# One table of issue orders for five engines: attention and two dense layers fused on one core

## The chip, the core and the metric

The kernel runs on one core of a Trainium2 chip. The core has five engines with a queue of instructions each: TensorE (PE in the profile), VectorE (DVE), ScalarE (ACT), GpSimd (POOL) and SyncE (SP), which issues every DMA of this kernel. An engine takes its instructions in the order in which they stand in its queue, and each of them waits on semaphores for what it reads and for the buffer it overwrites. The metric is the device time of one execution in microseconds (us); lower is better.

## The reference

```python
k_p = k.reshape(B, H, Sp, 8, D).mean(axis=3)          # B, H, S, D = 8, 8, 576, 64
v_p = v.reshape(B, H, Sp, 8, D).mean(axis=3)          # Sp = 72
scores = scale * np.matmul(q, k_p.transpose(0, 1, 3, 2))
attn = softmax(scores)
x = np.matmul(attn, v_p) -> reshaped to (4608, 512)   # one row for each token

h = x @ w_in                                          # 512 x 1024
solu = h * softmax(h)
ln = (solu - mean) / sqrt(var + 1e-06) * g_ln
x = ln @ w_out                                        # 1024 x 512

a, b = x @ w1, x @ w2                                 # 512 x 1024 each
out = (a * b) @ w3 @ w_out2                           # 1024 x 1024, 1024 x 512
```

## The kernel before

The program has two parts. The first holds the attention, the layer with `w_in` and `w_out`, and the conversion of `w1` and `w2`. It is cut into 18 units of 256 tokens, and each unit into 16 slots of PE work (`HEAVY = "hhhhxxxxHHHHyyyy"`: h chunks are products with `w_in`, L718; x chunks are products with `w_out`, L812 to L814). The attention of later tokens lies between them: scores `sc` (L582), maxima (L600), exponentials (L603), the division (`pr`, L623 and L630), transposes `pt` and `px` (L648, L651), and the product with the values, `av` (L687). Matrix products are made of a high and a low half of each operand (`xh` and `xl`, `gwh` and `gwl`, `pth` and `ptl`), so that each product is three matmuls.

q blocks come in 16 DMAs for each group of tokens (`qb`, L554), keys and values in `kv` tiles (L406, their remainder L414). The weights come as 64-bit words and are rounded to 32 bits by integer operations. A piece of 128 x 512 words is loaded into one of two buffers `f64` (`w_out` at L325, `w1` and `w2` at L247, "Kept" pieces; `w_in`, at the start, has six). POOL takes its low words (`cvm`, L258), ACT its magnitude (`cvb`, L260), DVE puts the bits together in three instructions (L263, L264, L267), and POOL adds the two (L273). A load into `f64` waits for L267 of the piece two before it. The 16 Kept pieces of `w1` and `w2` are then written back to DRAM (L359). `w_out` is centred over its rows: of each half of its columns four pieces are summed over the rows on PE (`nm`, L349), and L337 subtracts from it before it is split in `gwh` and `gwl`. The rows `h` go through `e` (L727, L733), are turned by PE (`lt`, L798) or through DRAM (`turn`, `ed`, `back`; L742, L749, L756), and each result `xo` is stored to `x2d` (L825).

The second part reads `x2d` back and forms `a` and `b` with seven products per block in place of eight (`p`, L1118 to L1120; their partial sums go to DRAM as `pd`, L1111), multiplies `w3` by `w_out2` (`ow`, L1277 to L1279), and ends in the last products (`o`, L1356 to L1358). `split` at L185 and L186 makes the high and the low half of an operand.

What sets the order: in the first part PE and SP issue in the order of the code (`manual_schedule` over the two), and DVE, ACT and POOL by the table `ISSUE_ORDER`, a list of offsets. In the second part all five engines issue in the order of the code. Nothing else is free: the tiles, the buffers and the operations are written out. Each DMA of SP also waits for the one that stands eight places before it in SP's queue, since eight semaphores take turns.

Of the kernel before, what the change touches and what calls it, by code (L numbers as in the profile page):

```python
# [1513 lines left out]
```

## Time and profile before

| | |
|---|---|
| three runs | 1217.00, 1218.17 and 1221.26 us, median 1218.17 us |
| profiled execution | 1221.05 us, its trace spans 1219.2 us |
| PE busy | 1163.4 us, 95% of the span |
| DVE, ACT, POOL busy | 895.7, 537.4, 522.5 us (73%, 44%, 43%) |
| DMA | 178.56 MB, mean 146 GB/s |
| granted clock of PE | 0.989 of full speed in the mean |

The span goes from the first to the last instruction. PE's 5% of idle time and its granted clock are where a change of order can act: the work itself stays. "SPq" in a view is SP's queue of DMAs. The clock of a stretch is the mean of two levels, full speed (2.4 GHz) and half of it.

### The profile page before, as it was taken

How to read it: one execution, taken by the hardware profiler on the slowest of the kernel's cores; microseconds unless marked ns; L12 is line 12 of the kernel's file. 1: busy time of each engine (PE TensorE's matmuls, PEld its weight loads, DVE VectorE, ACT ScalarE, POOL GpSimd, SP SyncE). 2: the span in 40 equal slices, each digit the busy share in tenths (PEclk: the TensorE clock that was granted, in tenths of full speed). 3: DMA queues.
4: the chain of work that ended last, by engine and by line, in shares of the span. 5: the costliest groups of instructions: out<-in, count | busy, mean ns of one | idle time of the engine just before them, and what ended most of it. 6: DMA issues, size and time to landing. Idle time of an engine off the chain costs nothing. (4 is left out here: it accounts for less than half of the span.)

```text
span 1219.2 us, 20186 instructions
## 1 busy us (share of the span) xinstructions
PE 1163.4 (95%) x7218; PEld 1037.5 (85%) x7218; DVE 895.7 (73%) x1376; ACT 537.4 (44%) x1399; POOL 522.5 (43%) x482
## 2 busy tenths in 40 slices
PE   7767999899999989999999999999999999999998
PEld 5656988788999989999999888888878887999997
DVE  6748777877887768658758977978784647877776
ACT  5544655565656566645533113131120224454534
POOL 3424333443344334200028657767672214645451
PEclk9989999999999999999999999999999999999999
DMA  9544255667677666435531642635612362153532
GB/s 234 116 113 96 70 126 139 187 163 192 168 193 204 173 146 197 127 133 184 176 126 61 220 164 98 205 130 180 201 61 86 121 216 86 49 195 122 181 131 87
DMA packets 167205, 178.56 MB, mean 146 GB/s; under 512 B 82624, under 2 KB 107200, under 8 KB 167104
## 3 DMA queue, kind: packets, MB, share of 16 engines
q1 hardware_dynamic: 167104, 177.26, 49.3%
q8 instruction: 57, 0.93, 0.3%
q14 instruction: 44, 0.36, 0.1%
HBM read 114.30 MB, written 62.91 MB: 145 GB/s over the span
## 5 line engine op out<-in xcount | busy, mean ns | idle before, releaser
L812 PE MATMUL x<-lnh,gwh 128*128 128x256 f32 x576 | 167.0, 290 | 0.0
L814 PE MATMUL x<-lnh,gwl 128*128 128x256 f32 x576 | 164.1, 285 | 0.0
L813 PE MATMUL x<-lnl,gwh 128*128 128x256 f32 x576 | 164.0, 285 | 0.0
L812 PEld LDWEIGHTS x<-lnh,gwh 128*128 128x128 f32 x576 | 111.1, 193 | 1.0 <-DVE lnl L802 0.2
L813 PEld LDWEIGHTS x<-lnl,gwh 128*128 128x128 f32 x576 | 111.2, 193 | 0.9
L603 ACT ACTIVATE ea<-sc,mx 128x72 f32<-128x72 f32 x320 | 98.0, 325 | 30.8 <-DVE mx L600 28.4
L814 PEld LDWEIGHTS x<-lnh,gwl 128*128 128x128 f32 x576 | 111.1, 193 | 0.0
L1122 ACT ACTIVATE p<-p 128x512 f32<-128x512 f32 (+1 forms) x40 | 22.2, 554 | 171.7 <-PE p L1120 165.1
L718 PE MATMUL h<-winh,xh 128*128 128x512 f32 x288 | 94.6, 410 | 1.8 <-DVE e L733 1.8
L1134 POOL TENSOR_TENSOR a<-a,b 128x512 f32<-128x512 f32 (+1 forms) x40 | 54.6, 1366 | 83.4 <-issue 57.3
L718 PE MATMUL h<-winl,xh 128*128 128x512 f32 x288 | 89.9, 393 | 0.0
L718 PE MATMUL h<-winh,xl 128*128 128x512 f32 x288 | 89.4, 392 | 0.0
L623 POOL TENSOR_TENSOR pr<-ea,sm 128x512 f32<-128x512 f32 x40 | 44.1, 1103 | 97.9 <-DVE sm L619 72.0
L727 ACT ACTIVATE e<-h,ST 128x1024 f32<-128x1024 f32 x36 | 40.2, 1116 | 64.8 <-DVE ST L726 64.5
L603 ACT ACTIVATION_READ_ACCUMULATOR ea<-sc,mx 128x1 f32 x320 | 67.8, 212 | 0.0
L718 PEld LDWEIGHTS h<-winh,xl 128*128 128x128 f32 x288 | 54.4, 189 | 12.1
L718 PEld LDWEIGHTS h<-winl,xh 128*128 128x128 f32 x288 | 54.4, 189 | 12.1
L1364 ACT ACTIVATE rows<-rows,kap 128x512 f32<-128x512 f32 x36 | 24.1, 716 | 90.3 <-DVE rows L1403 86.5
L1120 PE MATMUL p<-th,w1l 128*128 128x512 f32 (+1 forms) x160 | 59.4, 371 | 0.0
L1119 PE MATMUL p<-th,w1h 128*128 128x512 f32 (+1 forms) x160 | 59.1, 369 | 0.3 <-POOL th L1064 0.3
L1118 PE MATMUL p<-th,w1h 128*128 128x512 f32 (+1 forms) x160 | 59.3, 371 | 0.0
L1157 ACT ACTIVATE xq<-xq 128x512 f32<-128x512 f32 x24 | 16.2, 673 | 94.3 <-DMA xq<-in_moe_w_dram 65.8
(281 smaller groups left out, 3843.5 us busy)
## 6 DMA issues: line engine op xcount, KB each, us to landing
raw<-pd SPq DMA_DIRECT2D x18, 1024.0 KB
pd<-a SPq DMA_DIRECT2D x64, 256.0 KB
ed<-turn SPq DMA_DIRECT2D x28, 512.0 KB
back<-ed SPq DMA_DIRECT2D x112, 128.0 KB
x2d<-xo SPq DMA_DIRECT2D x35, 256.0 KB
kv<-in_k_dram SPq DMA_DIRECT2D x32, 256.0 KB
kv<-in_v_dram SPq DMA_DIRECT2D x32, 256.0 KB
f<-in_moe_w_dram SPq DMA_DIRECT2D x16, 512.0 KB
```

What stands on the lines that cost most here:

```text
L603: nc.scalar.activation(e[0:n, x], half[a][:, h], AF.Exp, bias=mx[0:n, x : x + 1], scale=1.0, accum_out=sm[0:n, x : x + 1],)
L623: nc.gpsimd.tensor_tensor(pr[0:n, 0 : H * KM].rearrange("p (h k) -> p h k", h=H), e[0:n, :, 0:KM], s8.to_broadcast([n, H, KM]), ALU.mult,)
L718: nc.tensor.matmul(self.ph[:, a], s_[:, c], w_[:, c, a * 512 : a * 512 + 512], start=first, stop=last)
L727: nc.scalar.activation(self.e, self.hv, AF.Exp, bias=st[:, 0:1], scale=1.0, accum_out=st[:, 1:2])
L812: nc.tensor.matmul(o, gw[0][:, f, ws], self.th[:, f], start=(f == 0), stop=False)
L813: nc.tensor.matmul(o, gw[0][:, f, ws], self.tl[:, f], start=False, stop=False)
L814: nc.tensor.matmul(o, gw[1][:, f, ws], self.th[:, f], start=False, stop=(f == FC - 1))
L1118: nc.tensor.matmul(o, wh[:, c, fsl], th[:, c], start=c == 0, stop=False)
L1119: nc.tensor.matmul(o, wh[:, c, fsl], tl[:, c], start=False, stop=False)
L1120: nc.tensor.matmul(o, wl[:, c, fsl], th[:, c], start=False, stop=c == 1)
L1134: nc.gpsimd.tensor_tensor(a[:, 0], a[:, 0], b[:, 0], ALU.mult)
L1364: nc.scalar.activation(dst, src, AF.Copy, scale=kap[:, n : n + 1])
```

## The change

The table now holds all five engines and the whole program, and the two `manual_schedule` blocks are gone. Its form is new too: runs of consecutive instructions (skip so many, take so many) in place of offsets. `issue_order` is called once, at the end, and chains the instructions of each engine in the table's order.

```diff
 def issue_order(tc, first):
     ins = list(tc.nc.cur_bb.bb.instructions)[first:]
     info = mybir.DependencyInfo(mybir.DependencyClass.NoSync, mybir.DependencyReason.DATA)
-    for engine, moves in ISSUE_ORDER.items():
-        traced = [i for i in ins if i.engine == getattr(mybir.EngineType, engine)]
-        order = [traced[k + m] for k, m in enumerate(moves)]
+    for engine, runs in ISSUE_ORDER.items():
+        traced = [i for i in ins if i.engine == getattr(mybir.EngineType, engine) and "Tile" not in type(i).__name__]
+        order, at = [], 0
+        for run in runs.split():
+            skip, _, count = run.partition(":")
+            at += int(skip)
+            order += traced[at : at + int(count or 1)]
+            at += int(count or 1)
+        assert len(order) == len(traced)
         for earlier, later in zip(order, order[1:]):
             tc.add_manual_dep(later, earlier.name, info, reason="issue order")
...
+    "SP": (
+        "0:2 2:2 -3 -2 3:3 1 -2 1 2 -3:2 5:2 -4:2 -4:2 4:6 2:2 -4:2 7:4 -9 8:8 4 -5:4 -20:4 17:2 3 -4 3:4 "
...
-    with tc.manual_schedule(engines={mybir.EngineType.PE, mybir.EngineType.SP}):
-        for s_ in range(min(events), SLOTS * (NU + 1) + 10):
+    for s_ in range(min(events), SLOTS * (NU + 1) + 10):
...
-    issue_order(tc, first_ins)
...
-    with tc.manual_schedule(engines={E.PE, E.SP, E.Activation, E.DVE, E.Pool}):
-        ON_POOL = (1, 3, 5)
+    ON_POOL = (1, 3, 5)
...
+    issue_order(tc, first_ins)
```

The instructions are the same ones on each engine: 6946 on PE, 1340 on DVE, 1007 on ACT, 485 on POOL and 792 on SP. On PE 344 of them stand in another place, nearly all in the first 245 us; on DVE 1196, on ACT 843, on POOL 359 and on SP 732. The new file is 25 to 28 lines longer, so L325 reads L352 there, L349 L376, L554 L581 and so on.

Three places, each of before and then of the change. The first is SP's queue at some 46 to 80 us, around the q blocks of the third group (`qb2`), the values of the second batch (`kv1_0`, `kv1_1`, `vl1`) and the pieces of `w_out` (`f64`). Before:

```order
26 L406 DMA kv1_0_635<-in_v_dram 64x2x512 x2
27 L414 DMA vl1_638<-in_v_dram 64x1x512 x2
28 L554 DMA qb2_641<-in_q_dram 32x8x32 x16
29 L325 DMA f64_683<-in_moe_w_out_dram 128x2x512
30 L406 DMA kv1_1_707<-in_v_dram 64x2x512 x2
31 L325 DMA f64_742<-in_moe_w_out_dram 128x2x512
32 L325 DMA f64_792<-in_moe_w_out_dram 128x2x512
33 L325 DMA f64_898<-in_moe_w_out_dram 128x2x512
34 L554 DMA qb3_928<-in_q_dram 32x10x32 x16
35 L325 DMA f64_989<-in_moe_w_out_dram 128x2x512
```

And now (`f64_681` is the piece that was `f64_683`; `f64_896` and `f64_987` were 898 and 989):

```order
27 L581 DMA qb2_639<-in_q_dram 32x8x32 x8
28 L352 DMA f64_681<-in_moe_w_out_dram 128x2x512
29 L581 DMA qb2_639<-in_q_dram 32x8x32 x4
30 L433 DMA kv1_0_633<-in_v_dram 64x2x512 x2
31 L441 DMA vl1_636<-in_v_dram 64x1x512 x2
32 L433 DMA kv1_1_705<-in_v_dram 64x2x512 x2
...
39 L581 DMA qb4_1294<-in_q_dram 32x8x32 x14
40 L433 DMA kv2_0_1141<-in_k_dram 64x2x512 x2
...
44 L441 DMA vl2_1291<-in_v_dram 64x1x512 x2
45 L352 DMA f64_896<-in_moe_w_out_dram 128x2x512
46 L352 DMA f64_987<-in_moe_w_out_dram 128x2x512
```

The q blocks and the fourth piece of `w_out` went ahead of the values of the second batch, and the last two pieces of `w_out` went behind the next group's q blocks and the third batch's keys.

The second place is PE's queue at some 112 to 130 us, at the row sums `nm` of the second half of `w_out`. Before:

```order
200 L349 MATMUL nm_1147<-cvb_820,gT_79 128x256 x2
201 L349 MATMUL nm_1147<-cvb_911,gT_79 128x256 x2
202 L349 MATMUL nm_1147<-cvb_1005,gT_79 128x256 x2
203 L349 MATMUL nm_1147<-cvb_1075,gT_79 128x256 x2
204 L812 MATMUL x2_0_0_1080<-lnh0_803,gwh_108 128x256
...
216 L687 MATMUL av2_2_1169<-pth2_953,VBDh_112 128x256
...
228 L718 MATMUL h1_1_1201<-winh_106,xh1_836 128x512 x2
```

And now, with the same names two or so lower:

```order
222 L376 MATMUL nm_1145<-cvb_818,gT_79 128x256 x2
223 L376 MATMUL nm_1145<-cvb_909,gT_79 128x256 x2
224 L714 MATMUL av2_2_1167<-pth2_951,VBDl_113 128x256
...
237 L745 MATMUL h1_1_1199<-winh_106,xh1_834 128x512 x2
238 L609 MATMUL sc3_0_1_1186<-bdt1_111,qT3_0_1070 128x144 x2
239 L376 MATMUL nm_1145<-cvb_1003,gT_79 128x256 x2
240 L745 MATMUL h1_1_1199<-winl_107,xh1_834 128x512 x2
...
245 L376 MATMUL nm_1145<-cvb_1073,gT_79 128x256 x2
246 L745 MATMUL h1_1_1199<-winh_106,xl1_835 128x512
```

The four pairs of sums stood in one row ahead of the x and h products; now the x products, `av2` and part of `h1_1` stand ahead of the third and the fourth pair.

The third place is DVE's queue at some 195 to 205 us of before, where the attention of the sixth group (`mx5`, `sm5`, `ptl5`) runs. Before, with one piece's conversion (`cvb_2127`) in it:

```order
259 L726 TENSOR_REDUCE ST_77<-h3_1_1982 128x1
260 L600 TENSOR_REDUCE mx5_1_2088<-sc5_1_0_2040 128x4
261 L438 TENSOR_REDUCE kp3_1_2147<-kv3_1_1979 128x128
262 L733 SCALAR_TENSOR_TENSOR e3_1_2031,ST_77<-h3_1_1982,e3_1_2031 128x1024
263 L600 TENSOR_REDUCE mx5_1_2088<-sc5_1_1_2043 128x4
264 L659 TENSOR_TENSOR ptl5_2115<-pt5_0_2117,pth5_2114 128x4x128
265 L660 TENSOR_TENSOR ptx5_2116<-px5_0_2122,ptx5_2116 64x128
266 L263 TENSOR_SCALAR cvb_2127<-cvb_2127 128x512
267 L742 STREAM_TRANSPOSE turn3_1_2063<-e3_1_2031 128x8x4x32
```

And now, from the same reduction of `h3_1` on:

```order
275 L753 TENSOR_REDUCE ST_77<-h3_1_1980 128x1
276 L627 TENSOR_REDUCE mx5_1_2086<-sc5_1_0_2038 128x4
277 L590 STREAM_TRANSPOSE qT6_1_2290<-qb6_2069 128x512
278 L290 TENSOR_SCALAR cvb_3304<-cvb_3304 128x512
279 L627 TENSOR_REDUCE mx5_1_2086<-sc5_1_1_2041 128x4
280 L291 TENSOR_SCALAR cvb_3304<-cvb_3304 128x512
281 L760 SCALAR_TENSOR_TENSOR e3_1_2029,ST_77<-h3_1_1980,e3_1_2029 128x1024
282 L686 TENSOR_TENSOR ptl5_2113<-pt5_0_2115,pth5_2112 128x4x128
283 L645 TENSOR_SCALAR sm5_1_2087<-sm5_1_2087 128x8
284 L646 RECIPROCAL sm5_1_2087<-sm5_1_2087 128x8
285 L294 SCALAR_TENSOR_TENSOR cvb_3304<-f64_3204,cvb_3304 128x512
```

The piece in this place is now a later one (3304; it was 3306, and DVE took it up at 304.7 us in before's trace, four pieces after 2127), and `qT6_1` came ahead by some rows. All 16 Kept pieces are taken up earlier in this way, at places that DVE reached by 275 us in before's trace, where the last of them was taken up at 502 us.

## Rows read from the trace of the kernel before

**Rows 1.** The page: PE's busy time, and DVE in 40 equal slices of the span.

```profile
PE 1163.4 (95%) x7218; PEld 1037.5 (85%) x7218; DVE 895.7 (73%) x1376; ACT 537.4 (44%) x1399; POOL 522.5 (43%) x482
...
DVE  6748777877887768658758977978784647877776
```

**Rows 2.** What PE waited for: total us, times, longest us.

```profile
PE nm L349 <- POOL cvb L273: 12.2, 2, 6.6
PE pkm L453 <- DMA kv<-in_k_dram: 7.3, 2, 6.4
...
PE sc L582 <- DVE xl L186: 3.2, 1, 3.2
PE w L313 <- DVE VBDl L186: 2.9, 1, 2.9
PE vs L444 <- DMA kv<-in_v_dram: 2.7, 1, 2.7
```

**Rows 3.** Stretches: length, busy us of each engine, PE's clock, DMA share, GB/s.

```profile
0.00:60.00 60.00, 46.36 (x248) 35.33 (x249) 41.49 (x83) 30.48 (x99) 23.57 (x42) 0.97 0.77 178
60.00:75.00 15.00, 12.85 (x83) 10.89 (x81) 6.86 (x20) 9.42 (x40) 5.02 (x10) 1.00 0.47 87
75.00:150.00 75.00, 60.63 (x366) 54.61 (x364) 56.75 (x112) 38.30 (x133) 26.55 (x34) 0.91 0.37 93
150.00:242.00 92.00, 85.43 (x564) 77.47 (x563) 68.67 (x128) 53.49 (x189) 38.74 (x55) 1.00 0.59 149
242.00:320.00 78.00, 74.64 (x496) 68.89 (x496) 56.82 (x95) 46.33 (x155) 26.02 (x37) 0.98 0.67 177
320.00:600.00 280.00, 276.55 (x1844) 255.53 (x1843) 206.26 (x346) 166.12 (x502) 83.03 (x117) 0.99 0.60 169
600.00:1000.00 400.00, 396.57 (x1980) 331.57 (x1979) 296.83 (x434) 93.51 (x147) 219.18 (x152) 1.00 0.43 144
1000.00:1050.00 50.00, 46.84 (x270) 40.06 (x269) 35.94 (x46) 24.12 (x43) 20.99 (x9) 0.97 0.26 85
```

**Rows 4.** POOL at 76 to 86 us: start, us, operation, idle time before.

```profile
80.17 0.66 POOL L258 TENSOR_SCALAR cvm<-f 128x512 int32<-128x512 uint32 x1 [7.82 <-DMA f<-in_moe_w_out_dram]
82.58 1.26 POOL L273 TENSOR_TENSOR cvb<-cvb,cvm 128x512 int32<-128x512 int32 x1 [1.76 <-DVE cvb L267]
```

**Rows 5.** SP's DMA issues at 46 to 84 us, then at 84 to 160 us.

```profile
64.67 10.28 SPq L554 DMA_DIRECT2D qb<-in_q_dram  x16
75.06 0.39 SPq L325 DMA_DIRECT2D f<-in_moe_w_out_dram  x1
...
111.13 0.40 SPq L325 DMA_DIRECT2D f<-in_moe_w_out_dram  x1
```

**Rows 6.** What SP's queue waited for at 40 to 160 us.

```profile
SPq L325 <- DVE cvb L267: 30.1, 3, 17.7
SPq L406 <- PE sc L582: 15.5, 1, 15.5
```

**Rows 7.** DVE at 75 to 242 us by form: count, busy us, mean ns.

```profile
L267 DVE SCALAR_TENSOR_TENSOR cvb<-f,cvb 128x512 int32<-128x512 int32 x10 | 7.3, 734 | 0.3
...
L264 DVE TENSOR_SCALAR cvb<-cvb 128x512 int32<-128x512 int32 x10 | 5.3, 526 | 0.3
...
L263 DVE TENSOR_SCALAR cvb<-cvb 128x512 f32<-128x512 f32 x10 | 4.2, 424 | 3.7 <-ACT cvb L260 3.5
```

**Rows 8.** The waits at 424 to 436 us.

```profile
POOL cvm L258 <- DMA f<-in_moe_w_dram: 9.9, 1, 9.9
...
DVE cvb L263 <- ACT cvb L260: 3.8, 1, 3.8
```

**Rows 9.** DVE, then POOL, at 1010 to 1026 us.

```profile
1012.47 2.60 DVE L186 TENSOR_TENSOR wcl<-wf,wch 128x256 fp32r<-128x256 f32 x1
...
1019.53 0.41 DVE L186 TENSOR_TENSOR wcl<-ow,wch 128x256 fp32r<-128x256 f32 x1
...
1012.37 2.41 POOL L1340 TENSOR_TENSOR s<-raw,raw 128x1024 f32<-128x1024 f32 x1
```

More of the change, by code (lines that the diff above doesn't have):

```diff
@@ L999, in attention_moe_kernel @@
     first_ins = len(nc.cur_bb.bb.instructions)
-    with tc.manual_schedule(engines={mybir.EngineType.PE, mybir.EngineType.SP}):
-        for s_ in range(min(events), SLOTS * (NU + 1) + 10):
-            now = s_
-            for _, _, fn, args in sorted(events.pop(s_, []), key=lambda e: e[:2]):
-                fn(*args)
-            u, c = s_ // SLOTS, s_ % SLOTS
-            kind, n = HEAVY[c], c % 4
-            for i, first in enumerate(H0):
-                if first <= s_ < first + 4:
-                    units[0].rows[i].chunk(s_ - first)
-            if kind in "hH" and 0 < u < NU:
-                units[u].rows["hH".index(kind)].chunk(n)
-            elif kind in "xy":
-                cp = "xy".index(kind)
-                if 0 <= u - 1 < AT_ONCE:
-                    units[u - 1].chunk(cp, n)
-                elif cp == 1 and AT_ONCE <= u - 1 < NU:
-                    units[u - 1].chunk(0, n)
-                elif cp == 0 and AT_ONCE <= u - 2 < NU:
-                    units[u - 2].chunk(1, n)
-        assert not events
-        now = None
-        mlp.close()
-        XA = ctx.enter_context(tc.tile_pool(name="xa", bufs=1, reuse_waits="tile"))
-        TH = [XA.tile([P, 2048], F32R, tag=f"th{i}", name=f"th{i}") for i in range(7)]
-        xqs = ExitStack()
-        XB = xqs.enter_context(tc.tile_pool(name="xb", bufs=1, reuse_waits="tile"))
-        XQ = [XB.tile([P, 1024], F32, tag=f"xq{i}", name=f"xq{i}") for i in range(7)]
-        class Blocks:
-            def __init__(self, js, slots):
-                self.js, self.slots, self.w = js, slots, 256 * len(js)
-                self.ready, self.n = [], 0
-            def load(self):
-                if len(self.js) == 2:
-                    self.b = [x.rearrange("p (c n) -> p c n", c=2) for x in XQ]
-                    for i, (r, h) in enumerate(((0, 0), (0, 1), (1, 1), (1, 0))):
-                        for g in range(2):
-                            nc.sync.dma_start(self.b[i][:, :, g * U : g * U + U], x2d[self.js[h], g, r])
-                b11, b12, b22, b21, t1, t2, t4 = self.b
-                self.todo = [b11, t2, t1, b21, b12, t4, b22]
-            def sums(self, i):
-                difference(self.b, i)
-            def slot(self, k):
-                if len(self.js) == 2:
-                    return TH[self.slots[k]].rearrange("p (t c n) -> p t c n", t=2, c=2)
-                t = TH[self.slots[k // 2]][:, k % 2 * 1024 : k % 2 * 1024 + 1024]
-                return t.rearrange("p (t c n) -> p t c n", t=2, c=2)
-            def hi(self):
-                k = len(self.ready)
-                t = self.slot(k)
-                nc.scalar.activation(t[:, 0], self.todo[k], AF.Copy)
-                self.ready.append((t[:, 0], t[:, 1]))
-            def lo(self):
-                i, self.n = self.n, self.n + 1
-                h, l = self.ready[i]
-                eng = nc.gpsimd if i in ON_POOL else nc.vector
-                eng.tensor_tensor(l, self.todo[i], h.bitcast(F32), ALU.subtract)
-        ON_POOL = ()
-        xs = Blocks((0,), (0, 1, 2, 3))
-        xs.b = first_x
-        xs.load()
-        for k in range(7):
-            xs.hi()
-            xs.lo()
-        units[-1].store(1)
-        out_scale()
@@ L1075, in attention_moe_kernel @@
-    issue_order(tc, first_ins)
+    for s_ in range(min(events), SLOTS * (NU + 1) + 10):
+        now = s_
+        for _, _, fn, args in sorted(events.pop(s_, []), key=lambda e: e[:2]):
+            fn(*args)
+        u, c = s_ // SLOTS, s_ % SLOTS
+        kind, n = HEAVY[c], c % 4
+        for i, first in enumerate(H0):
+            if first <= s_ < first + 4:
+                units[0].rows[i].chunk(s_ - first)
+        if kind in "hH" and 0 < u < NU:
+            units[u].rows["hH".index(kind)].chunk(n)
+        elif kind in "xy":
+            cp = "xy".index(kind)
+            if 0 <= u - 1 < AT_ONCE:
+                units[u - 1].chunk(cp, n)
+            elif cp == 1 and AT_ONCE <= u - 1 < NU:
+                units[u - 1].chunk(0, n)
+            elif cp == 0 and AT_ONCE <= u - 2 < NU:
+                units[u - 2].chunk(1, n)
@@ new lines, in attention_moe_kernel, with __init__, load, sums @@
+    assert not events
+    now = None
+    mlp.close()
+    XA = ctx.enter_context(tc.tile_pool(name="xa", bufs=1, reuse_waits="tile"))
+    TH = [XA.tile([P, 2048], F32R, tag=f"th{i}", name=f"th{i}") for i in range(7)]
+    xqs = ExitStack()
+    XB = xqs.enter_context(tc.tile_pool(name="xb", bufs=1, reuse_waits="tile"))
+    XQ = [XB.tile([P, 1024], F32, tag=f"xq{i}", name=f"xq{i}") for i in range(7)]
+    class Blocks:
+        def __init__(self, js, slots):
+            self.js, self.slots, self.w = js, slots, 256 * len(js)
+            self.ready, self.n = [], 0
+        def load(self):
+            if len(self.js) == 2:
+                self.b = [x.rearrange("p (c n) -> p c n", c=2) for x in XQ]
+                for i, (r, h) in enumerate(((0, 0), (0, 1), (1, 1), (1, 0))):
+                    for g in range(2):
+                        nc.sync.dma_start(self.b[i][:, :, g * U : g * U + U], x2d[self.js[h], g, r])
+            b11, b12, b22, b21, t1, t2, t4 = self.b
+            self.todo = [b11, t2, t1, b21, b12, t4, b22]
+        def sums(self, i):
+            difference(self.b, i)
+        def slot(self, k):
+            if len(self.js) == 2:
+                return TH[self.slots[k]].rearrange("p (t c n) -> p t c n", t=2, c=2)
+            t = TH[self.slots[k // 2]][:, k % 2 * 1024 : k % 2 * 1024 + 1024]
+            return t.rearrange("p (t c n) -> p t c n", t=2, c=2)
+        def hi(self):
+            k = len(self.ready)
+            t = self.slot(k)
+            nc.scalar.activation(t[:, 0], self.todo[k], AF.Copy)
+            self.ready.append((t[:, 0], t[:, 1]))
+        def lo(self):
+            i, self.n = self.n, self.n + 1
+            h, l = self.ready[i]
+            eng = nc.gpsimd if i in ON_POOL else nc.vector
+            eng.tensor_tensor(l, self.todo[i], h.bitcast(F32), ALU.subtract)
@@ L1076, in attention_moe_kernel @@
+    ON_POOL = ()
+    xs = Blocks((0,), (0, 1, 2, 3))
+    xs.b = first_x
+    xs.load()
+    for k in range(7):
+        xs.hi()
+        xs.lo()
+    units[-1].store(1)
+    out_scale()
     raws.close()
@@ L1411, in use @@
                     self.store(i)
-    E = mybir.EngineType
-    with tc.manual_schedule(engines={E.PE, E.SP, E.Activation, E.DVE, E.Pool}):
-        ON_POOL = (1, 3, 5)
-        slots = [4, 5, 6, 7, 0, 1, 2]
-        spare = 3
-        for n in range(5):
-            if n < 4:
-                nxt = Blocks((2 * n + 1, 2 * n + 2), tuple(slots))
-                steps = plan(nxt, [])
-            else:
-                nxt = None
-                steps = mid_steps()
-            if 0 < n < 4:
-                part = late[8 * (n - 1) : 8 * n]
-                for pc in part:
-                    pc.__class__ = Late
-                for key, st in plan(None, part).items():
-                    steps.setdefault(key, [])[:0] = st
-            for fc in range(FC):
-                ab(xs, fc, steps)
-            if nxt is not None:
-                xs = nxt
-                if n < 3:
-                    slots, spare = [spare] + slots[:6], slots[6]
-        products.close()
-        sums.close()
-        RB = ctx.enter_context(tc.tile_pool(name="last", bufs=1, side="right", reuse_waits="tile"))
-        BK = [RB.tile([P, 2048], F32R, tag=f"bk{i}", name=f"bk{i}") for i in range(6)]
-        BK += [TH[i] for i in (spare, slots[0], slots[1], slots[5])]
-        wc = weight_pair(wp, "w16", [P, 4, F], "wc")
-        last = [Last(j) for j in range(NB)]
-        z = last[0]
-        early = {
-            1: [(z.load, 0)],
-            2: [(z.load, 1)],
-            3: [(z.split, 0)],
-            4: [(z.sum, "s1"), (z.sum, "s2"), (z.split, 3), (last[1].load, 0)],
-            5: [(z.sum, "s3"), (z.sum, "s4"), (last[1].load, 1)],
-            6: [(z.split, 1)],
-            7: [(z.split, 2), (last[1].sum, "s1")],
-        }
-        for n in range(FC):
-            for i in range(2):
-                if n + 2 < FC:
-                    load_w3(n + 2, i)
-            for i in range(2):
-                if n + 1 < FC:
-                    w3_T(n + 1, i)
-            ow = wf_rows(n)
-            if n % 2 == 0:
-                w12, t1 = upper(n // 2, ow)
-            else:
-                lower(n // 2, ow, w12, t1)
-            for fn, *args in early.get(n, ()):
-                fn(*args)
-        stg.close()
-        OT = ctx.enter_context(tc.tile_pool(name="out", bufs=1, reuse_waits="tile"))
-        for j, un in enumerate(last):
-            n1_, n2_ = [last[i] if i < NB else None for i in (j + 1, j + 2)]
-            for n in range(7):
-                if n == 0 and n2_:
-                    n2_.load(0)
-                    n2_.load(1)
-                if n1_ and n in (0, 2, 4):
-                    n1_.sum(("s2", "s3", "s4")[n // 2])
-                if n == 6 and n2_:
-                    n2_.sum("s1")
-                if un is z and n < 3:
-                    z.split(4 + n)
-                if n1_:
-                    n1_.split(n1_.order[n])
-                un.product(n)
@@ new lines, in attention_moe_kernel @@
+    ON_POOL = (1, 3, 5)
+    slots = [4, 5, 6, 7, 0, 1, 2]
+    spare = 3
+    for n in range(5):
+        if n < 4:
+            nxt = Blocks((2 * n + 1, 2 * n + 2), tuple(slots))
+            steps = plan(nxt, [])
+        else:
+            nxt = None
+            steps = mid_steps()
+        if 0 < n < 4:
+            part = late[8 * (n - 1) : 8 * n]
+            for pc in part:
+                pc.__class__ = Late
+            for key, st in plan(None, part).items():
+                steps.setdefault(key, [])[:0] = st
+        for fc in range(FC):
+            ab(xs, fc, steps)
+        if nxt is not None:
+            xs = nxt
+            if n < 3:
+                slots, spare = [spare] + slots[:6], slots[6]
@@ new lines, in attention_moe_kernel @@
+    products.close()
+    sums.close()
+    RB = ctx.enter_context(tc.tile_pool(name="last", bufs=1, side="right", reuse_waits="tile"))
+    BK = [RB.tile([P, 2048], F32R, tag=f"bk{i}", name=f"bk{i}") for i in range(6)]
+    BK += [TH[i] for i in (spare, slots[0], slots[1], slots[5])]
+    wc = weight_pair(wp, "w16", [P, 4, F], "wc")
+    last = [Last(j) for j in range(NB)]
+    z = last[0]
+    early = {
+        1: [(z.load, 0)],
+        2: [(z.load, 1)],
+        3: [(z.split, 0)],
+        4: [(z.sum, "s1"), (z.sum, "s2"), (z.split, 3), (last[1].load, 0)],
+        5: [(z.sum, "s3"), (z.sum, "s4"), (last[1].load, 1)],
+        6: [(z.split, 1)],
+        7: [(z.split, 2), (last[1].sum, "s1")],
+    }
@@ new lines, in attention_moe_kernel @@
+    for n in range(FC):
+        for i in range(2):
+            if n + 2 < FC:
+                load_w3(n + 2, i)
+        for i in range(2):
+            if n + 1 < FC:
+                w3_T(n + 1, i)
+        ow = wf_rows(n)
+        if n % 2 == 0:
+            w12, t1 = upper(n // 2, ow)
+        else:
+            lower(n // 2, ow, w12, t1)
+        for fn, *args in early.get(n, ()):
+            fn(*args)
+    stg.close()
+    OT = ctx.enter_context(tc.tile_pool(name="out", bufs=1, reuse_waits="tile"))
@@ new lines, in attention_moe_kernel @@
+    for j, un in enumerate(last):
+        n1_, n2_ = [last[i] if i < NB else None for i in (j + 1, j + 2)]
+        for n in range(7):
+            if n == 0 and n2_:
+                n2_.load(0)
+                n2_.load(1)
+            if n1_ and n in (0, 2, 4):
+                n1_.sum(("s2", "s3", "s4")[n // 2])
+            if n == 6 and n2_:
+                n2_.sum("s1")
+            if un is z and n < 3:
+                z.split(4 + n)
+            if n1_:
+                n1_.split(n1_.order[n])
+            un.product(n)
```

2 lines of the change are left out of this document (added), and 147 rows, old and new, of the table ISSUE_ORDER.

## Prediction

> **What bounds the kernel now.** The page comes first. PE is busy for 1163.4 of 1219.2 us [rows 1], so at most 55.8 us of idle time and what the clock costs can be saved; no instruction is added or taken away. The question is how much of that hangs on order, and where.
>
> The windows say where it lies [rows 3]. From 320 to 1000 us PE is busy for 276.55 + 396.57 of 680 us, 0.990 of the time: that is as dense as this kernel runs, and I call it full pace. From 75 to 150 us it is 60.63 of 75 us, and the granted clock there is 0.91, so the busy time itself contains work at half speed: a mean of 0.91 over 75 us means 6.8 us lost to the lower level (the mean's deficit times the length). Taking that off, a stage at full pace would need (busy - clock loss) / 0.990:
>
> 0 to 60 us: loss 0.03 x 60 = 1.8, so 44.6 / 0.99 = 45.0 us, 15 less than it takes; but nothing can run until the first loads are in.
> 60 to 75: 13.0, 2.0 less.
> 75 to 150: 53.8 / 0.99 = 54.4, 20.6 less.
> 150 to 242: 86.3, 5.7 less.
> 242 to 320: loss 1.6, 73.8, 4.2 less.
> 320 to 600: the clock's row of 0.99 is rounded, so the loss is 1.4 to 4.2; some 3 to 5 less.
> 600 to 1000: none less, by definition.
> 1000 to 1050: loss 1.5, 45.8, 4.2 less.
>
> The rest of the span, 169 us, keeps nearly its old order and is taken as unchanged.
>
> Then the chain of waits, which says what ends last in each of these stages [rows 2]. The largest entry is 12.2 us in two waits for `nm`, the row sums of `w_out`: PE stands for the last piece of each half. The reader should follow one of them back. POOL began that piece at 80.17 us after 7.8 us without work, waiting for a DMA, and added its halves from 82.58 to 83.84 us [rows 4]; PE went on at about that time. The load itself was issued at 75.06 us, directly behind 10.28 us of q block issues (16 of them) [rows 5]. And these were late because SP had stood 15.5 us at the load of the second batch's values, whose buffer PE's scores still held back [rows 6]. So PE waited not for a transfer's length, but for an issue that stood in SP's queue behind another's wait. The second half went the same way: three loads of L325 stood 30.1 us, the longest 17.7, for the conversion two pieces before [rows 6], 16 q blocks stood behind the longest, and the eighth piece was issued at 111.13 us [rows 5]. The other entries here, apart from the start, are single waits of 2 to 3 us. The low clock belongs to the stalls: 0.91 in the stage with the two `nm` waits, 1.00 in those before and after it [rows 3].
>
> **The change part by part.**
>
> *75 to 242 us, the main term.* In SP's queue the fourth piece of `w_out` and `qb2` now stand ahead of the values whose buffer is late (first place shown). Nothing else held the fourth piece: without the 15.5 us of waiting it can be issued some 13 us earlier, and its conversion on POOL, ACT and DVE went forward as well. That takes away the first 6.6 us wait whole. Pieces seven and eight did not go forward: they stand behind `qb4` and the keys of batch 2. For them the change works on the other side: two of the four pairs of row sums moved behind x products, `av2` and chunks of `h1` (second place). The fourth pair stands 43 matmuls later than before; at 85.43 us for 564 of them, the pace of the stage after [rows 3], these are 6.5 us of PE work, and the wait that they are to cover is 12.2 - 6.6 = 5.6 us. With both stalls their half clock goes too. What is left is a floor set by PE, 54.4 + 86.3 = 140.7 us for 167, or 26.3 us to gain.
>
> But there is a second floor. DVE is busy for 56.75 + 68.67 = 125.4 us of these 167 [rows 3]. I added up, with the durations of before's trace, what stands in DVE's new order between the instructions at which PE now passes the places of 75 and 242 us: 136.6 us, 11 more. It is 4 to 5 Kept pieces at 0.73 + 0.53 + 0.42 = 1.68 us each [rows 7], which used to be converted later (third place), and transposes of q. So DVE becomes nearly as full as PE. How full can it run? No window here has it over 0.76, but one slice of the page has a 9, 90% or more over 30 us [rows 1], while PE was at full pace. I take 0.92: 136.6 / 0.92 = 148 us, so **19 us saved**. The bounds: at 0.85 it is 160 us, 7 saved; if DVE does not bind, 26 saved.
>
> *0 to 60 us.* The keys go ahead of the first piece of `w_in`, and four loads of values ahead of two others, for which PE waits 7.3 us (6.4 of it the very start) and 2.7 us; `VBDl`, for which it waits 2.9 us, is taken ahead of two conversions on DVE [rows 2]. With the 1.8 us of clock that is at most 7.4 us without the start. The DMA share is 0.77 in this stage [rows 3], so whatever goes forward pushes other loads back: half, **4 us** (0 to 8).
>
> *60 to 75 us.* The attention's small operations go ahead of conversions on DVE: **1 us** (0 to 2).
>
> *242 to 320 us.* The waits here are short ones for DVE, and by now the conversions are 12.6 us ahead of their former place on DVE, so it is no lighter: **3 us** (1 to 4).
>
> *320 to 600 us.* One wait stands out, 3.2 us of `sc` for `xl` [rows 2]. A late piece caused it: POOL waited 9.9 us for a load and DVE then 3.8 us for ACT's share of it [rows 8], with the attention's `xl` standing behind it. With the half clock that followed (1.5 us) it cost 4.7 us. The Kept pieces are all converted well ahead of this place now, by 275 us in place of 502, so this goes: **4 us** (1 to 5). From 600 to 1000 us PE is at full pace and nothing is taken from it: **0** (0 to 2).
>
> *1000 to 1050 us.* The product of `w3` and `w_out2`. DVE's split of `wcl` is reordered there against POOL's sums. The same operation takes 0.41 us alone and 2.60 us where a sum of 2.41 us runs on POOL beside it [rows 9], and PE's waits follow it. The new order could place these apart; that costs or gains a few us: **2** (0 to 4).
>
> *What the change adds.* Stores of `x2d`, `w1f` and `ed` move back by 19 to 58 places in SP's queue, so their buffers come free later; and many loads are pulled forward and may meet full transfers. No row prices that; I set **-2 us** (0 to -5).
>
> Sum: 19 + 4 + 1 + 3 + 4 + 0 + 2 - 2 = 31 us. The profiled execution took 1221.05 us, so 1190; it lies 2.9 us above the median of the three runs shown (1218.17), and the median of the new ones should be about **1187 us**. All upper ends together are 26 + 8 + 2 + 4 + 5 + 2 + 4 = 51, 1167 us in the median; all lower ends 7 + 0 + 0 + 1 + 1 + 0 + 0 - 5 = 4, 1214 us.
>
> **The rivals.**
>
> *DVE and POOL block one another (0.20).* The rows just read show a DVE operation with two inputs stretched by 2.2 us, about the length of POOL's, when they overlap [rows 9]. POOL's own work between 75 and 242 us is also pulled forward, by 12.7 us up to 236 us by the durations of before. If every one of these microseconds stops DVE, its 136.6 become 149.3, at 0.92 162 us, and 19 us saved become 5; with the same in 242 to 320 us (0 for 3) the sum is 31 - 17 = 14, a median of 1204 us. For it: DVE would be the fuller engine. Against it: L267 has two inputs and runs in this very stage beside POOL's conversions, and its mean over ten is 0.73 us [rows 7], so none of them stood for long.
> The Trainium skill, "SBUF — State Buffer", section "Who interferes with whom", says that a DVE operation in a two-port mode or with two inputs in SBUF and a GpSimd operation that reads SBUF lock one shared port pair for their whole length. The row of 2.60 us agrees with it; by that rule the table's price would be what this rival gives, about 1204 us.
>
> *A late piece in front (slower, 0.11).* About 11 Kept pieces are pulled forward between 130 and 275 us, each with three DVE instructions in front of attention work that PE needs. DVE takes nothing out of turn: where the piece's load lands late, the attention behind it stands. The row of 424 us is just this, at 4.7 us for one piece. At 31 / 4.7, some 7 pieces late, the gain is gone; with 8 of 11 the sum is 31 - 38 = -7, 1225 us. For it: loads of this stage share the queue with 0.59 to 0.67 of the DMA engines' time [rows 3]. Against it: their loads are also issued earlier, by up to 200 places.
>
> *The table changes nothing that ends last (0.07).* The `nm` waits could simply become waits for the piece after, since SP's 8-place limit holds issues back as well. Then only the small terms 1 and 2 stay: 1215 to 1217 us.
>
> **How the numbers follow.** The forecast has 0.62, so the likeliest time is 1187 us, with 1174 to 1200 as its own range. To leave out no more than 2 in 10, the range takes in the first rival and the lower ends: 1170 to 1213 us. Faster by over 0.3% (under 1214.5 us; 0.3% is about what a measurement of this kernel can tell) has the forecast, the first rival and none of the others, 0.81 to 0.82; within 0.3% the last rival with a bit, 0.08; slower 0.11.
>
> **What would show it.** In the new profile the chain of waits should have no `nm` entry over 1 us, and the windows of 75 to 150 us a clock of 0.97 or more. PE should reach the instruction that it starts at 242 us in before's trace at some 217 to 222 us. DVE's busy share up to there should be 0.88 to 0.95. If the first rival holds, L267, L186 or L659 take visibly longer in that stage than in before's rows; if the second, PE's waits name `xl`, `ptl` or `mx` on DVE, and DVE's own waits name `cvb` on ACT or a load `f`. The prediction would be wrong in its main step if `nm` stays, or if its time reappears as waits for `pt` or `sc` before 320 us.

## The result and the profile after

The changed kernel takes 1185.0 us (1183.89 to 1189.36, four runs), the kernel before 1219.72 us (1217.0 to 1222.02, four runs). The ratio is 0.972, with a 95% interval of 0.969 to 0.976: faster by 2.8%, where 1187 us had been forecast. The profiled execution took 1183.89 us, its span is 1182.1 us.

The page, as in [rows 1]: PE's busy share went from 95 to 98%, DVE's from 73 to 79%.

```profile
PE 1153.5 (98%) x7218; PEld 1028.0 (87%) x7218; DVE 929.1 (79%) x1376; ACT 540.5 (46%) x1399; POOL 528.9 (45%) x482
...
DVE  5899889988777775686669869879784667999982
```

What PE waited for, over the whole span, as in [rows 2]:

```profile
PE pkm L480 <- DMA kv<-in_k_dram: 6.0, 1, 6.0
PE ow L1302 <- ACT th L212: 1.9, 1, 1.9
PE w L340 <- DVE cvb L330: 1.8, 3, 1.2
PE lt L825 <- DVE lnl L829: 1.8, 2, 1.0
PE ow L1304 <- DVE th L213: 1.7, 1, 1.7
PE x L839 <- ACT lnh L815: 1.5, 1, 1.5
```

The 12.2 us for `nm` are gone, and nothing of that size took their place: after the start (`pkm`) no wait is longer than 1.9 us. The stages are best compared by the work done, not by the clock. PE's order is nearly the same in both kernels, so I count its matmuls: 326 of them start before 74.7 us in the trace of before, 1254 before 242 us, and so on. The rows of after are cut where PE starts the same matmuls as before at 60, 74.7, 150, 242, 320, 600, 1000 and 1050 us (columns as in [rows 3]):

```profile
0.00:56.00 56.00, 46.11 (x248) 33.47 (x249) 38.87 (x81) 29.97 (x98) 22.70 (x40) 1.00 0.78 198
56.00:67.90 11.90, 11.90 (x81) 10.56 (x80) 9.80 (x23) 9.95 (x41) 8.03 (x12) 1.00 0.90 192
67.90:125.60 57.70, 56.19 (x367) 50.44 (x366) 56.06 (x112) 38.55 (x136) 29.46 (x41) 1.00 0.62 139
125.60:215.80 90.20, 85.97 (x564) 77.35 (x563) 80.95 (x144) 56.27 (x194) 50.28 (x66) 1.00 0.74 203
215.80:289.00 73.20, 73.11 (x496) 67.33 (x495) 63.21 (x107) 46.77 (x158) 40.34 (x50) 1.00 0.83 215
289.00:566.00 277.00, 275.28 (x1845) 254.03 (x1844) 192.83 (x319) 165.01 (x499) 58.77 (x88) 1.00 0.49 142
566.00:964.60 398.60, 396.10 (x1981) 331.76 (x1980) 306.07 (x433) 92.34 (x143) 223.01 (x154) 1.00 0.44 146
964.60:1013.80 49.20, 45.62 (x270) 40.01 (x269) 42.26 (x51) 25.32 (x43) 27.45 (x12) 0.97 0.25 86
```

| stage of before, us | took | takes now | saved | forecast |
|---|---|---|---|---|
| 0 to 60 | 60.1 | 56.0 | 4.1 | 4 |
| 60 to 74.7 | 14.6 | 11.9 | 2.7 | 1 |
| 74.7 to 150 | 75.5 | 57.7 | 17.8 | 19 with the next |
| 150 to 242 | 91.9 | 90.2 | 1.7 | |
| 242 to 320 | 78.0 | 73.2 | 4.8 | 3 |
| 320 to 600 | 279.9 | 277.0 | 2.9 | 4 |
| 600 to 1000 | 400.1 | 398.6 | 1.5 | 0 |
| 1000 to 1050 | 49.9 | 49.2 | 0.7 | 2 |
| rest | 169.2 | 168.3 | 0.9 | 0, and -2 for what is added |

The two spans differ by 37.1 us and the medians by 34.7 us; the profiled execution of the changed kernel was the fastest of its four. The stage from 74.7 to 242 us now takes 147.9 us where 148 had been forecast, and DVE is busy for 56.06 + 80.95 = 137.0 us of it, 0.926 of the time, where 136.6 and 0.92 had been forecast. That agreement is what the experiments put to the test.

### The profile page after: what moved, and what is told of

Read it like the earlier page. It is cut to its first block, busy times and chain, and to the rows that moved or that the text cites. A ratio compares the mean times of both kernels' runs of the same rounds, so it can differ in the third digit from the quotient of the medians.

```text
span 1182.1 us, 20238 instructions
## 1 busy us (share of the span) xinstructions
PE 1153.5 (98%) x7218; PEld 1028.0 (87%) x7218; DVE 929.1 (79%) x1376; ACT 540.5 (46%) x1399; POOL 528.9 (45%) x482
## 5 line engine op out<-in xcount | busy, mean ns | idle before, releaser
L1159 POOL TENSOR_TENSOR a<-a,b 128x512 f32<-128x512 f32 (+1 forms) x40 | 51.6, 1289 | 112.8 <-issue 69.9
L760 DVE SCALAR_TENSOR_TENSOR e<-h,e 128x1024 f32<-128x1024 f32 x36 | 44.0, 1222 | 17.2 <-ACT e L754 16.9
L745 PEld LDWEIGHTS h<-winh,xh 128*128 128x128 f32 x288 | 50.2, 190 | 7.9 <-issue 1.3
```

Source lines behind the costliest of these rows:

```text
L745: nc.tensor.matmul(self.ph[:, a], s_[:, c], w_[:, c, a * 512 : a * 512 + 512], start=first, stop=last)
L1159: nc.gpsimd.tensor_tensor(a[:, 0], a[:, 0], b[:, 0], ALU.mult)
```

## The experiments

Each run was timed beside the kernel before on the same chip, whose median was 1218.3 to 1219.2 us each time. "Stage" is the time from the 326th to the 1254th matmul, "242 to 450" the time from there to the matmul that before starts at 450 us (167.4 and 207.9 us in before, 147.9 and 198.9 in the changed kernel). Both come from one profiled execution, and the changed kernel's second profile (e4) shows 150.1 and 199.0, with 3.4 us of the stage at half clock where the first has none, so a difference of 2 us in a stage tells little.

| run | median us | ratio to before, interval | stage | 242 to 450 |
|---|---|---|---|---|
| before, one load forward (e1) | 1217.82 | 1.000, 0.997 to 1.002 | 165.2 | 206.1 |
| and its conversion forward (e2) | 1211.18 | 0.992, 0.990 to 0.995 | 160.9 | 206.8 |
| e2, and nm later on PE (e8) | 1210.32 | 0.994, 0.992 to 0.996 | 157.8 | 207.5 |
| e2, and two POOL operations exchanged (e12) | 1208.38 | 0.991, 0.989 to 0.994 | 156.2 | 204.3 |
| before, Kept pieces forward (e11) | 1233.47 | 1.012, 1.009 to 1.014 | 181.1 | 206.2 |
| new order in part one alone (e3) | 1186.5 | 0.971, 0.968 to 0.974 | 149.7 | 199.5 |
| changed kernel again (e4) | 1185.73 | 0.973, 0.969 to 0.976 | 150.1 | 199.0 |
| less DVE work (e5) | 1184.97 | 0.973, 0.969 to 0.977 | 146.3 | 198.8 |
| more DVE work (e6) | 1190.86 | 0.977, 0.974 to 0.981 | 151.2 | 202.3 |
| less POOL work (e7) | 1187.03 | 0.974, 0.970 to 0.977 | 149.9 | 198.5 |
| changed kernel, Kept pieces back (e9) | 1196.65 | 0.983, 0.980 to 0.985 | 146.3 | 210.7 |
| changed kernel, Kept pieces half way (e10) | 1200.44 | 0.986, 0.983 to 0.988 | 149.9 | 211.6 |

**e1: one load, on SP alone.** The line numbers in this and the next diffs are those of the kernel that ran, some 18 below before's; `f_681` is the fourth piece of `w_out`.

```diff
 L307 DMA f_573<-in_moe_w_out_dram 128x2x512
+L307 DMA f_681<-in_moe_w_out_dram 128x2x512
 L388 DMA kv_0_633<-in_v_dram 64x2x512 x2
 L396 DMA vl_636<-in_v_dram 64x1x512 x2
 L536 DMA qb_639<-in_q_dram 32x8x32 x16
-L307 DMA f_681<-in_moe_w_out_dram 128x2x512
```

> The order of before with one move: on SP the load of the fourth piece of w_out goes ahead of the loads of the second batch's values. My reading of the prediction (SP's queue is what made the piece late): the first wait for nm, 6.6 us, goes with its half clock of 3.4 us, 1208 to 1211 us in place of 1218. Rival: the conversion's own places on DVE, ACT and POOL hold it as well, DVE had the operation before it until 79.2 us and PE went on at 84, so at most 1 to 3 us are saved, 1215 to 1218 us, and the wait for nm stays at 4 us or more.

The rival held: no change that can be measured, and at 60 to 100 us PE still waits 4.4 us for `nm`:

```profile
PE nm L331 <- POOL cvb L255: 4.4, 1, 4.4
```

The timelines of POOL, ACT and DVE show why (start, us, operation, idle before it):

```profile
72.58 0.65 POOL L240 TENSOR_SCALAR cvm<-f 128x512 int32<-128x512 uint32 x1
80.50 1.26 POOL L255 TENSOR_TENSOR cvb<-cvb,cvm 128x512 int32<-128x512 int32 x1 [7.27 <-DVE cvb L249]
...
77.20 0.65 ACT L242 ACTIVATE cvb<-f 128x512 f32<-128x512 f32 x1
...
77.62 1.19 DVE L715 SCALAR_TENSOR_TENSOR e<-h,e 128x1024 f32<-128x1024 f32 x1
...
78.74 0.42 DVE L245 TENSOR_SCALAR cvb<-cvb 128x512 f32<-128x512 f32 x1
```

The piece was there 8 us earlier: POOL took its low words at 72.58 us, without idle time before it, in place of 80.17 [rows 4]. But on ACT its magnitude (L242) still stood behind the exponential of the rows `h`, and on DVE its conversion (L245) behind `e` of the same rows, until 78.74 us. The load was only the later of two things that were late at the same place.

**e2: the conversion too.** On DVE it goes ahead of the reduction of the same rows `h`, on ACT and POOL likewise.

```diff
+L245 TENSOR_SCALAR cvb<-cvb 128x512
+L246 TENSOR_SCALAR cvb<-cvb 128x512
+L249 SCALAR_TENSOR_TENSOR cvb<-f_681,cvb 128x512
 L708 TENSOR_REDUCE ST<-h_1_731 128x1
 L545 STREAM_TRANSPOSE qT_0_757<-qb_639 128x512
 L545 STREAM_TRANSPOSE qT_1_815<-qb_639 128x512
 L715 SCALAR_TENSOR_TENSOR e_1_783,ST<-h_1_731,e_1_783 128x1024
-L245 TENSOR_SCALAR cvb<-cvb 128x512
-L246 TENSOR_SCALAR cvb<-cvb 128x512
-L249 SCALAR_TENSOR_TENSOR cvb<-f_681,cvb 128x512
```

> As the run before, and the fourth piece's conversion goes forward too: on ACT ahead of the exponential of the second row block, on DVE ahead of its reduction, on POOL ahead of the values' sums. Both readings: the first wait for nm is gone, PE is 8 to 10 us earlier at 90 us. If the second wait for nm (5.6 us) keeps its size, the total is 1208 to 1211 us. Rival: its load waits for conversions that do not move, so the second wait grows by what the first one gave, and the total stays at 1215 to 1219 us.

As both readings had it: 7.8 us in the medians, and one `nm` wait where there were two. What PE waited for at 100 to 150 us:

```profile
PE nm L331 <- POOL cvb L255: 6.5, 1, 6.5
```

**e8 and e12: the second wait.** In e8 PE alone is changed: the four pairs of the second `nm` go where the changed kernel has them.

```diff
-L331 MATMUL nm<-cvb,gT 128x256 x8
...
+L331 MATMUL nm<-cvb,gT 128x256 x4
...
+L331 MATMUL nm<-cvb,gT 128x256 x2
...
+L331 MATMUL nm<-cvb,gT 128x256 x2
```

> As the run with the fourth piece moved on all engines (1211 us), and on PE the four pairs of the second nm go to their new places, 14, 34 and 43 matmuls later. My reading: the matmuls in front cover the second wait of 6.5 us and its half clock of 3.4 us, 1201 to 1204 us, PE some 17 us earlier than before at the matmul that before started at 150 us. Rival: a wait for gwh or gwl of the second half takes its place, since what follows nm is as late as it was: 1207 to 1212 us.

The rival again: the time is that of e2 (the intervals overlap). The wait for `nm` is gone, and these stand in its place at 104 to 150 us:

```profile
PE sc L564 <- DVE xl L168: 2.6, 2, 1.9
PE x L796 <- DVE gwl L323: 1.2, 1, 1.2
PE pt L630 <- POOL pr L605: 0.8, 1, 0.8
```

What follows the row sums on DVE (the centring and the split into `gwl`, and `xl` between them) is as late as it was (the first `gwl` starts at 118.96 us, in e2 at 119.13), and PE meets it some matmuls further on. In e12 PE is as before, and on POOL the eighth piece's addition goes ahead of the first Kept piece's low words:

```diff
 L240 TENSOR_SCALAR cvm<-f_987 128x512
+L255 TENSOR_TENSOR cvb<-cvb,cvm 128x512
 L240 TENSOR_SCALAR cvm<-f_1021 128x512
-L255 TENSOR_TENSOR cvb<-cvb,cvm 128x512
```

> As the run with the fourth piece moved on all engines (1211 us), with two POOL instructions exchanged: the eighth piece's addition ahead of the first Kept piece's low words, for whose load POOL stood 4.3 us with the addition behind it. If that is a part of the second nm wait (6.5 us), it falls to 3 to 4 us, and the total to 1207 to 1209 us. Rival, DVE's share of the piece holds it anyway: 1210 to 1212 us, and the wait stays.

The wait is halved, as expected:

```profile
PE nm L331 <- POOL cvb L255: 3.3, 1, 3.3
```

So 3.2 us of the second stall came from an operation on POOL that waited for a load which nobody needed yet. The medians agree with it (2.8 us less than e2), but the intervals overlap, so the wait's row is the evidence.

**e3: which part of the program.** The table's first part new, everything after the layer with `w_out` in before's order.

> The new order in the first part alone (up to the end of the layer with w_out), the second part as before. The prediction gives the second part 2 of its 31 us, the stages of the two traces 3 of 37: 1186 to 1189 us. Rival: the second part's new order carries a third or more of the gain, hidden in the stages by earlier loads: 1195 us or more.

The whole gain is there; the second part's new order gives nothing that can be measured.

**e4 to e7: is DVE the limit of the stage?** e4 is the changed kernel itself.

> The changed kernel once more, as the measure for the three runs beside it: 1183 to 1190 us, the stage between the matmuls that before started at 74.7 and 242 us again 147 to 149 us.

The time came out as expected, 1185.73 us; the stage took 150.1 us, 1 us more than expected.

In e5 each Kept piece has one DVE instruction less, in e6 one more:

```diff
-            nc.vector.tensor_scalar(b, b, 3, 0x3FFFFFFF, ALU.logical_shift_left, ALU.bitwise_and)
+            if not isinstance(self, Kept):
+                nc.vector.tensor_scalar(b, b, 3, 0x3FFFFFFF, ALU.logical_shift_left, ALU.bitwise_and)
...
             nc.vector.tensor_scalar(b, b, 3, 0x3FFFFFFF, ALU.logical_shift_left, ALU.bitwise_and)
+            if isinstance(self, Kept):
+                nc.vector.tensor_scalar(b, b, 0, 0x3FFFFFFF, ALU.logical_shift_left, ALU.bitwise_and)
```

> The changed kernel without one of the three DVE instructions of each Kept piece (the shift of L291, so w1 and w2 come out as other numbers). Ten of them at 0.68 us lie in the stage, 6.8 us of DVE's 136.6. If DVE binds the stage at 0.926, it goes from 147.5 to PE's floor of 141 to 142 us, and the total falls by 5 to 6 us. Rival, DVE is full there but PE's losses are waits for single results: 1 us or less.

> The changed kernel with one more DVE instruction for each Kept piece (a second mask, which changes no value), ten in the stage, 5 to 7 us of DVE more. If DVE binds: 143 / 0.926 = 154 to 155 us for the stage, the total up by 6 to 7 us. Rival, DVE does not bind: up by 0 to 2 us.

e5 goes the rival's way: the total is the same (1184.97 against 1185.73 us). DVE is busy for 130.3 us of the stage in place of 137.0, and the stage takes 146.3 us, 1.6 less than in the first profile of the changed kernel, which has no half clock there either; DVE as the limit was to give 6. e6 lies between the two readings. With 7.0 us more (eleven second masks at 68 to 218 us) the total is 5.1 us longer: all six times lie above the six of e4, though the intervals of the two ratios still touch. Only 1 to 3 us of it are in the stage, and 3.3 us come between 242 and 450 us. So DVE's work is not the floor that I took it for; why work that is added costs time, where work that is taken away gives none, stays open.

In e7 the Kept pieces lose POOL's addition:

```diff
-            nc.gpsimd.tensor_tensor(self.b, self.b, self.m, ALU.add)
+            if type(self) is not Kept:
+                nc.gpsimd.tensor_tensor(self.b, self.b, self.m, ALU.add)
```

> The changed kernel without POOL's addition L300 for the 16 Kept pieces (the low words of w1 and w2 are left out). POOL has 10 x 1.37 = 13.7 us less in the stage. If POOL's work blocks DVE, the means of L290 and L291 there (0.605 and 0.679 us, in the kernel before 0.424 and 0.526) come back to those of before, DVE loses some 5 us and the stage 4 to 5 us. If not, the means stay and the total is within 1 us.

DVE by form at 68 to 218 us, first the changed kernel, then e7 (where L291 reads L286 and L290 L285):

```profile
L291 DVE TENSOR_SCALAR cvb<-cvb 128x512 int32<-128x512 int32 x15 | 10.2, 679 | 0.3
...
L290 DVE TENSOR_SCALAR cvb<-cvb 128x512 f32<-128x512 f32 x15 | 9.1, 605 | 3.8 <-ACT cvb L287 3.7
```

```profile
L285 DVE TENSOR_SCALAR cvb<-cvb 128x512 f32<-128x512 f32 x15 | 8.0, 530 | 3.9 <-ACT cvb L282 3.8
L286 DVE TENSOR_SCALAR cvb<-cvb 128x512 int32<-128x512 int32 x15 | 7.7, 511 | 0.3
```

The means do fall (L291 from 0.679 to 0.511 us, L290 from 0.605 to 0.530), together 3.6 us over fifteen of each; against e4, the second profile of the changed kernel (0.667 and 0.573), it is 3.0 us. So POOL's additions do lengthen DVE's operations, and the total does not notice (1187.03 against 1185.73 us). The stage settles nothing here: e7's profile has 6.8 us of it at half clock.

**e9 to e11: the Kept pieces.** In e9 and e10 fourteen of them are put back, whole and half way, in an order that is else the changed kernel's; in e11 all sixteen are put forward in before's order. I placed them by the times of the two traces alone, so what this placing costs by itself is not known. The piece that is `cvb_3304` in DVE's queue of the changed kernel stands beside `mx5` and `e3_1`; in e9 (whose lines are numbered 7 lower) it is back at `e7_0`, where before has it:

```diff
 L645 TENSOR_SCALAR sm5_1_2087<-sm5_1_2087 128x8
 L646 RECIPROCAL sm5_1_2087<-sm5_1_2087 128x8
-L294 SCALAR_TENSOR_TENSOR cvb_3304<-f64_3204,cvb_3304 128x512
...
 L746 TENSOR_REDUCE ST_77<-h7_0_3260 128x1
+L287 SCALAR_TENSOR_TENSOR cvb_3304<-f64_3204,cvb_3304 128x512
 L753 SCALAR_TENSOR_TENSOR e7_0_3317,ST_77<-h7_0_3260,e7_0_3317 128x1024
```

> The changed kernel with 14 of the 16 Kept pieces (loads, conversions and stores, all but the first two) put back to the places in the work where before had them. The stage up to the matmul of 242 us loses five pieces, some 10 us of DVE; after the runs on DVE I expect 2 to 4 us from that, and the wait at some 400 us, where a piece's load is late, back at 3 to 5 us: 1184 to 1190 us. Rival: pulling the pieces forward is what gives the 9 us between 242 and 450 us: 1192 to 1197 us.

> The same 14 pieces half way between their places in the two kernels. If both DVE's fullness before 216 us and late pieces after it cost something, this is the fastest: 1180 to 1184 us. Rival: neither is left as a cost, 1185 to 1188 us, as the changed kernel.

> The order of before with one part of the change: the 16 Kept pieces (loads, conversions, stores on SP, POOL, ACT and DVE) at the places in the work where the changed kernel has them. If pulling them forward is a gain by itself, the wait of 4.7 us at 424 us goes and more of the short waits between 242 and 450 us: 1208 to 1214 us. Rival, it is one only together with the rest of the new order, and on the old one the pieces stand in front of the attention at 150 to 275 us: 1216 us or more.

e9 is 11 us slower than the changed kernel, e10, of which both readings thought better, 15 us, and e11 is 15 us slower than before. In e9 and e10 the loss lies between 242 and 450 us (210.7 and 211.6 for 199 us), in e11 nearly all of it in the stage (181.1 for 167.4). Nearly the same move (14 pieces and 16) is a gain of 11 us in one order and a loss of 15 us in the other.

e9 also answers the question of DVE's limit once more. Its stage holds 14 us of DVE work less than the changed kernel's, and takes just as long as that of e5. The stage in e5, then in e9 (columns as in [rows 3]):

```profile
67.50:213.80 146.30, 141.74 (x929) 127.75 (x928) 130.33 (x244) 94.61 (x330) 79.40 (x106) 1.00 0.68 180
```

```profile
67.50:213.80 146.30, 141.46 (x929) 127.68 (x929) 123.20 (x239) 91.44 (x323) 65.76 (x95) 1.00 0.60 147
```

What PE waited for in e9 at 242 to 460 us, then in e10 at 217 to 430 us:

```profile
PE sc L602 <- DVE xl L206: 4.5, 2, 2.8
PE px L671 <- POOL pr L650: 1.7, 1, 1.7
PE pt L668 <- POOL pr L643: 1.5, 2, 0.8
```

```profile
PE pt L671 <- POOL pr L646: 5.5, 3, 3.5
PE px L674 <- POOL pr L653: 3.3, 3, 2.0
```

And all engines in e11 at 200 to 232 us:

```profile
POOL cvm L246 <- DMA f<-in_moe_w_dram: 10.4, 3, 6.5
DVE cvb L251 <- ACT cvb L248: 7.3, 2, 6.0
...
PE pt L636 <- POOL pr L611: 3.7, 2, 3.5
...
PE px L639 <- POOL pr L618: 3.0, 1, 3.0
```

e11 has the pattern of [rows 8], moved to another place: POOL stands for a piece's load, ACT and DVE for its magnitude, and the attention's `pr` behind them makes PE wait. The granted clock from before's place of 150 us to that of 242 us is 0.94, where before has 1.00, and PE's busy time in the stage grows from 146.5 to 152.4 us for the same matmuls. In the changed kernel POOL's waits for the loads of the same pieces are shorter in the stage, 3.2 us at most, and no PE wait there is over 1.5 us:

```profile
POOL cvm L285 <- DMA f<-in_moe_w_dram: 13.5, 7, 3.2
```

That these loads come in time because SP's queue was reordered with them is argued, not shown: no run moves the loads alone. Why half way (e10) is worse than either end is open.

## Why the prediction was right, and where only its number was right

**The size and the place** were right, stage by stage (the table above). Two stages gave a little more than their ranges: 2.7 us from 60 to 74.7 (0 to 2), 4.8 us from 242 to 320 (1 to 4). Of the signs that were named, no `nm` entry, a clock of 1.00 in the stages from 75 us to 1000 and DVE at 0.926 came; PE reached the place of 242 us at 215.8 us, just ahead of the 217 to 222 us that were named. The two `nm` stalls with their half clock are the core of it: 17.8 of 37.1 us are saved between 74.7 and 150 us, where PE now stands for 1.5 us in place of 14.4. Edits on before's order give 8 us of the gain by themselves (e2), and some 11 with e12, whose part is within the noise. The rest is placed by the two traces and by e3, not by single edits.

**"Nothing else held the fourth piece"** is the step that failed. e1 shows that the load alone, 8 us earlier, is worth nothing; e2 that load and conversion together are worth 8 us. I had followed the chain of waits back to SP and stopped there, though the queues of ACT and DVE held the piece until 78.7 us as well. The sum was saved because the change moves both.

**The matmuls in front of the second `nm`**, 6.5 us of them for a wait of 5.6 us, failed in the same way: e8 moves only PE and gains nothing that can be measured, since the results of the sums are late too. e12 adds what I had not seen, a POOL operation with an early wait ahead of the addition. The changed kernel has the addition and the matmuls in the better order; which of its further moves on DVE and ACT close the rest of this stall was not tried one by one.

**DVE as a floor at 0.92** gave 148 us, and 147.9 were measured, but the step does not hold. A floor would have let the stage of e5 and e9 fall to what PE needs; both stop at 146.3 us, with DVE at 0.89 and 0.84. PE's own floor was also set too low: 6.8 us were taken off its busy time for the half clock, though PE stood for a part of that time. Before's two stretches at half clock, columns as in [rows 3], have PE busy for 11.3 of 13.7 us:

```profile
82.56:89.39 6.83, 5.49 (x21) 5.02 (x21) 2.83 (x7) 2.13 (x8) 2.56 (x3) 0.50 0.23 77
120.11:126.93 6.82, 5.85 (x23) 5.49 (x24) 3.53 (x6) 1.11 (x2) 2.68 (x5) 0.50 0.01 5
```

Now, at full clock, PE is busy for 56.19 us of the stage from 74.7 to 150 us in place of 60.63 [rows 3], 4.4 less. By the prediction's own rule the floor of the whole stage up to 242 us is then (56.19 + 85.97) / 0.990 = 143.6 us and not 140.7. So 4.3 us of the 147.9 lie above it: single waits of a few tenths to 1.5 us for results of ACT, DVE and POOL. That these come more often when the three engines are full is likely, but not shown. The 0.92 came from a row of tenths (it has two 9s, not one), and that it hit is luck.

**The 4 us at 320 to 600 us**, put down to the pieces being early, were 2.9 us. e9 agrees that early is a gain in the new order (11 us), e11 shows that it is none by itself. As far as these runs go, the gain belongs to the order as a whole: loads, conversions and attention of one time. The second part's 2 us were 0.7, and no stage shows what I had set for moved stores and loads (-2).

**The rivals.** DVE and POOL do block one another, as e7's rows show; the additions of the Kept pieces cost 3.0 to 3.6 us of DVE time and nothing measurable of the kernel's, where the rival had 17 us. The operations that were named for it hardly moved (L267 from 0.734 to 0.752 us); one-input ones did. The two splits of [rows 9] were misread: the one of 0.41 us did not run alone, since a POOL sum ran from 1017.28 to 1020.64 us:

```profile
1017.28 3.36 POOL L1340 TENSOR_TENSOR s<-raw 128x1024 f32<-128x1024 f32 x1
```

It reads `ow`, a bank of matmul results (PSUM), where the one of 2.60 us reads `wf` in SBUF; so the two differ in their input, and not in whether POOL was busy. The Trainium skill, "SBUF — State Buffer", section "Who interferes with whom", names DVE operations in a two-port mode or with two inputs. By that rule L291, with one input in SBUF, would have to be the first of the two cases; no run here shows the mode. Beside POOL's addition L291 took 1.40 us where it takes 0.43 alone. The late piece in front, the rival on the other side, is real: e11 is 1.2% slower by it. It was at work in an order that I made, not in this table. The third rival, that a wait only moves to what comes next, is what e1 and e8 show of single moves; the whole table did not go that way.

The 4 us of the start (forecast 4) were not taken apart by a run.

## What to carry to other kernels

When a wait is followed back to a late transfer, ask at each engine on the way what else stands ahead of the same item, and how long it would stand there if the transfer were early: the second-latest thing sets the gain. An order table is worth what its engines do together; one part of it, taken alone, gave 0 (SP's in e1, PE's in e8) or a loss (the Kept pieces in e11), so a part is judged by running it with the others.

A busy share near one that fits the measured time is no proof of a limit. Take some work of that engine away, and add some: a limit answers to both.
